# Sixteen head pairs of a sparse attention in one hand order for all engines: two full-array visits per pair, K and Q rows cast once and placed by DMA between SBUF tiles

## The chip, the cores and the metric

The kernel runs on one core of one Trainium2 chip. The metric is device time in microseconds (us) of one execution. The engines are named as in the profile: PE is TensorE, DVE is VectorE, ACT is ScalarE, POOL is GpSimd and SP is the engine that only issues transfers.

## The reference

Attention with a selection of key chunks, then a mixture of experts with one expert per token. There are B=4 batches, H=8 heads, S=768 positions and D=64; 24 chunks of 32 keys, of which each query keeps six; E=8 experts with 512 to 1024 to 512 (N=3072 tokens).

```python
k_min = np.min(k_chunks, axis=3); k_max = np.max(k_chunks, axis=3)
ub = np.sum(np.maximum(q[..., None, :] * k_min, q[..., None, :] * k_max), axis=-1)
ub = np.where(causal, ub, -1e9)                 # by chunk
top_chunks = np.argsort(ub, axis=-1)[..., -6:]
scores = scale * q @ k.T
scores = np.where(sel & (i >= j), scores, -1e9) # sel: the chunk of j is kept
x = softmax(scores) @ v                         # [3072, 512] over all heads
logits = x @ w_gate
e = argmax(logits); g = softmax(logits)[e]
out = g * (relu(x @ w1[e]) @ w2[e])
```

## The kernel before

**Pairs.** The 32 heads are worked as NP=16 pairs; pair i is pair hp = i % 4 of batch b = i // 4. `load` brings q, k and v of a pair (fp32, 128 positions on the partitions). PE transposes K and Q so that the two heads lie on partitions 0 to 63 and 64 to 127. From K's transposes DVE takes each chunk's maximum and minimum (`kmx`, `kmn`), and `kse` makes their sum and difference (`KS`, `KD`). ACT writes K, scaled, into `KTE` as bf16, once for each head and half. `q_e` copies Q's transposes to `qT`, their absolute value to `qA`, and casts them into the rows 0 to 63 of `QSB`, head 0 on POOL and head 1 on ACT.

**Selection.** `ub` multiplies `KS` by `qT` and `KD` by `qA` (fp32, in 64-column tiles), which gives the upper bound of each chunk. Its transposes go to DVE (`select`), which takes the eight largest of each list with `max` and marks in `nsel` what is not among the six. `mask` transposes `nsel`, and ACT puts it in rows 64 to 87 of `QSB`. Rows 64 to 87 of `KTE` hold an indicator of the chunk, so one bf16 matmul over the whole array gives scores that are already masked.

**Scores and attend.** Scores are made transposed (keys on the partitions), in seven units u0 to u6: u0 and u1 are the first 384 queries, u2 to u6 the second 384. Each unit is one `scores` (PE, then exp on ACT into a tile `Pa` or `Pr`, then, on the diagonal, affine selects on POOL, L300) and one `attend` (PE, P times V into halves of 64 columns, fp32). DVE adds the units' P up in `acc` (L325), and copies the output `po` to `ot` (L318).

**Denominators and router.** `ud` of a pair (L341 and L346, 32-column tiles) makes from `acc` the softmax's denominators and from `ot` the pair's share of the router's logits. `lgp` transposes and divides these, `sums` adds the shares in `lg` on POOL, and `xr` transposes `ot`, scales it and writes it, as bf16, to `xrow`. After the last pair of a batch `route_steps` follow in the pairs of the next batch: `logits` (DVE), `rank` (PE and DVE), and six `scatter`s (POOL, indirect DMAs, L443) that write tokens to `xs_dram` by expert.

**Experts.** NA=11 tiles of 128 tokens are known early (`table`, over pairs 13 and 14), 28 tiles in all run. Each tile is gathered (POOL, L542), turned by a DMA transpose (`x_in`) into one of six slots in KTE[0] and QSB[0], then `up` (8 matmuls, Relu L592, a DMA transpose of h), and `down` (8 matmuls), scaling and an indirect DMA to the output. The second four gathers each reuse a buffer of the first four, whose transposes they wait for. The weights come as 32 pieces of 512 KB that POOL's queue casts to bf16 (`load_w`, L166).

**Order.** PE, POOL and SP run in the order in which the code lists instructions; DVE and ACT are left to the tile scheduler, apart from the start and from the last pair on, where they too run in the listed order. Within a pair there are four groups: scores u2 and u3; u4 and u5; u6; and, for the next pair, u0 and u1. After the scores of each group come the attends of the group before. `ub` follows the first group, `select` the second, `mask` the third and `lgp` and `x0` the fourth. The spread of scatters is a list, one or two to a group:

```python
spread = ((), (0,), (2, 4), (1,), (3, 5), (), (), ())
```

In the last pair the order of POOL is gathers 0 to 3, the affine selects of the groups as they come, and gathers 4 to 7 after scores u6.

## Time and profile before

| | |
|---|---|
| time, median of 3 executions | 370.18 us (369.44 to 373.85) |
| the profiled execution: its time | 363.95 us |
| the profiled execution: its span | 362.1 us |
| mean granted PE clock | 0.988 |
| busy PE / DVE / ACT / POOL | 93% / 64% / 65% / 49% |
| DMA packets, bytes, mean rate | 138215, 59.83 MB, 165 GB/s |
| first scores / first `up` | 16.73 us / 248.81 us |
| weight pieces, time from issue to landing (median) | 6.0 us |

The page has one row per engine of the busy share, with the number of instructions. In the slices each digit is the busy share of one fortieth of the span, in tenths, and PEclk is the clock that PE was granted. The profiled execution's time is that span with 1.85 us around it.

### The profile page before, as it was taken

What the parts mean: (1) busy time and instruction counts of PE and PEld (TensorE: products, weight loads), DVE (VectorE), ACT (ScalarE), POOL (GpSimd) and SP (SyncE); (2) the same over time, 40 slices, a digit from 0 to 9 for tenths busy, and PEclk for the clock granted to TensorE, in tenths of its full rate; (3) what the DMA queues carried; (4) which work ended last, traced back from release to release, by engine and by line L of the source; (5) the groups of instructions that cost most, each with busy time, mean ns of one, the idle gap of its engine ahead of it and who ended that gap; (6) DMA issues with size and microseconds to landing.
All of it is one profiled execution on the core that took longest, in us unless ns stands there. A gap on an engine that the chain in (4) does not pass through costs nothing. (4 is left out here: it accounts for less than half of the span.)

```text
span 362.1 us, 7547 instructions
## 1 busy us (share of the span) xinstructions
PE 335.4 (93%) x2312; PEld 173.4 (48%) x2312; DVE 232.1 (64%) x811; ACT 235.2 (65%) x398; POOL 177.1 (49%) x296
## 2 busy tenths in 40 slices
PE   6777999999999999999999997998999899999990
PEld 5534455465554554554545544443544344444440
DVE  5789788898998898998988999775370010000000
ACT  2496797797887977977879778462354445544450
POOL 3074333452476343457424538375576765555331
PEclk9999999999999999999999998999999999999996
DMA  7619997999948989957989992366999999999841
GB/s 148 114 24 198 201 206 113 217 194 177 219 108 185 191 121 195 205 123 193 167 138 201 183 186 67 83 125 121 164 193 236 204 245 211 215 197 193 175 123 51
DMA packets 138215, 59.83 MB, mean 165 GB/s; under 512 B 122811, under 2 KB 131005, under 8 KB 138176
## 3 DMA queue, kind: packets, MB, share of 16 engines
q1 hardware_dynamic: 119072, 29.52, 45.9%
q0 software_dynamic: 17536, 29.42, 42.0%
q10 hardware_dynamic: 1568, 0.39, 0.6%
q8 instruction: 21, 0.34, 0.4%
q14 instruction: 18, 0.15, 0.1%
HBM read 56.14 MB, written 10.51 MB: 184 GB/s over the span
## 5 line engine op out<-in xcount | busy, mean ns | idle before, releaser
L325 DVE TENSOR_TENSOR Pa<-Pa,Pr 128x768 f32<-128x768 f32 (+2 forms) x112 | 81.5, 728 | 1.8 <-DVE Pa L325 0.5
L300 POOL TENSOR_SCALAR_AFFINE_SELECT Pr<-Pr 128x256 f32<-128x256 f32 x80 | 31.9, 418 | 76.2 <-ACT Pr L296 75.3
L296 ACT ACTIVATE Pr<-ps 128x768 f32<-128x768 f32 (+2 forms) x112 | 65.0, 628 | 3.2 <-PE ps L291 2.9
L600 PE MATMUL py<-w_all,hT 128*128 x224 | 52.6, 379 | 1.0 <-DMA hT<-h__4066 0.8
L291 PE MATMUL ps<-QSB,KTE 128*128 128x384 bf16 (+2 forms) x288 | 49.1, 294 | 1.7 <-ACT QSB L265 1.2
L542 POOL DMA_INDIRECT xg<-xs_dram,grow x28 | 29.9, 1068 | 22.6 <-DVE gt_all L565 7.4
L563 DVE TENSOR_TENSOR ti_all<-xg,inv_i 128x1 int32<-128x1 int32 x17 | 2.8, 163 | 58.0 <-DMA xg<-xs_dram,grow 58.0
L291 PEld LDWEIGHTS <-KTE 128*128 128x128 bf16 x288 | 24.2, 98 | 32.6 <-issue 25.3
L608 POOL DMA_INDIRECT out_dram<-y,ti_all x28 | 27.8, 994 | 24.4 <-ACT y L607 18.7
L600 PEld LDWEIGHTS <-hT 128*128 128x128 bf16 x224 | 21.8, 98 | 27.6 <-DMA hT<-h__4066 1.2
L607 ACT ACTIVATE y<-py,gt_all 128x512 f32<-128x512 f32 x27 | 18.5, 687 | 20.6 <-PE py L600 19.9
L349 ACT ACTIVATE ud<-pu 128x384 f32<-128x384 f32 x16 | 7.9, 492 | 36.5 <-PE pu L346 36.5
L443 POOL DMA_INDIRECT xs_dram<-xrow,sli x24 | 26.9, 1121 | 6.6 <-issue 4.5
L589 PE MATMUL ph<-w_all,KTE 128*128 x120 | 28.4, 379 | 0.0
L296 ACT ACTIVATE Pa<-ps 128x768 f32<-128x768 f32 x32 | 26.0, 813 | 2.9 <-PE ps L291 2.3
L166 POOL DMA_DIRECT2D w_all<-in_moe_w_dram x32 | 24.4, 762 | 0.0
L300 POOL TENSOR_SCALAR_AFFINE_SELECT Pa<-Pa 128x256 f32<-128x256 f32 x16 | 6.5, 405 | 36.5 <-ACT Pa L296 36.5
L589 PE MATMUL ph<-w_all,QSB 128*128 x96 | 22.7, 379 | 0.2 <-issue 0.2
L379 DVE TENSOR_TENSOR xrow<-pt,rec 128x384 bf16<-128x384 f32 x32 | 17.6, 552 | 3.0 <-PE pu L236 1.7
L204 DVE TENSOR_REDUCE kmx<-pt 128x12 f32<-128x384 f32 x30 | 16.7, 556 | 4.0 <-PE pt L202 3.9
L221 POOL CAST QSB<-qT 64x384 bf16<-64x384 f32 x30 | 16.7, 564 | 4.1 <-DVE qT L219 2.7
L318 DVE COPY ot<-po 128x384 f32<-128x384 f32 x32 | 17.7, 553 | 1.2 <-PE po L313 1.2
(306 smaller groups left out, 639.5 us busy)
## 6 DMA issues: line engine op xcount, KB each, us to landing
w_all<-in_moe_w_dram POOLq DMA_DIRECT2D x32, 512.0 KB, 6.0
xg<-xs_dram,grow POOLq DMA_INDIRECT x28, 3.9
out_dram<-y,ti_all POOLq DMA_INDIRECT x28, 4.3
t__122<-in_k_dram SPq DMA_DIRECT2D x2, 192.0 KB, 3.5
t__125<-in_q_dram ACTq DMA_DIRECT2D x2, 192.0 KB, 4.0
t__128<-in_v_dram SPq DMA_DIRECT2D x2, 192.0 KB, 5.6
t__196<-in_k_dram SPq DMA_DIRECT2D x2, 192.0 KB
t__206<-in_q_dram SPq DMA_DIRECT2D x2, 192.0 KB, 3.7
```

Of the source, the lines that this page charges most:

```text
L166: nc.gpsimd.dma_start(out=dst, in_=src.rearrange("(c p) f -> p c f", p=128))
L291: nc.tensor.matmul(pv[:, hd, :], lhsT=kte[:, hd, ts(kb, 128)], rhs=qsb[:, hd, ds(qb * 384 + 384 - w, w)], start=True, stop=True, skip_grou ...
L296: nc.scalar.activation(P[:, :, ds(c0, w)], pv, AF.Exp)
L300: nc.gpsimd.affine_select(out=pd, in_=pd, pattern=[[0, 2], [1, 128]], compare_op=ALU.is_ge, fill=0.0, base=0, channel_multiplier=-1)
L318: nc.vector.tensor_copy(out=ot[:], in_=po[:])
L325: nc.vector.tensor_tensor(acc[:, :, 384 - w:384], acc[:, :, 384 - w:384], P[:, :, ds(c0, w)], ALU.add)
L443: d = nc.gpsimd.indirect_dma_start(out=xs_dram[:], out_offset=bass.IndirectOffsetOnAxis(ap=sli[:, u:u + 1], axis=0), in_=bst[b][f"xrow{u % ...
L542: d = nc.gpsimd.indirect_dma_start(out=xg_bufs[j % XB][:].bitcast(I32), out_offset=None, in_=xs_dram[:], in_offset=bass.IndirectOffsetOnAx ...
L589: nc.tensor.matmul(ph[:, fh, :], lhsT=xT[:, c, :], rhs=w_all[:, ds(wo + (c * F + fh * 512), 512)], start=(c == 0), stop=(c == NDC - 1), sk ...
L600: nc.tensor.matmul(py[:], lhsT=hT[:, c, :], rhs=w_all[:, ds(wo + (W1W + c * DM), DM)], start=(c == 0), stop=(c == NFC - 1))
L607: nc.scalar.activation(y[:], py[:], AF.Copy, bias=0.0, scale=fs[j]["gt"])
L608: d = nc.gpsimd.indirect_dma_start(out=out[:], out_offset=bass.IndirectOffsetOnAxis(ap=fs[j]["ti"], axis=0), in_=y[:], in_offset=None, bou ...
```

## The change

All five engines now run in one order that a function `iteration(i)` writes out. In an iteration, PE works on the scores of pair i, on u6's attend and the router's part of pair i-1, on the selection of pair i+1, and on the transposes of pair i+2. Scores u0, u1, u4 and u5 are split in two tiles of 64 columns (`split`), so that with the attends and `ub` they are of one mode; the whole array is used from q's transposes to u3, and from the masks to the transposes of x.

K and Q are cast once for both heads: K on ACT to `kB`, Q on POOL to `qB`; `rows` copies them by DMA to rows 0 to 63 of `KTE` and `QSB` (four DMAs per pair, on SP's queue). `kse` goes from DVE to POOL, the copy of the second output to ACT, and the exps of a unit of two parts become one. `ub` and the masks cover only the queries from 128 on (640 of 768); the earlier ones see at most four chunks and keep them all. Of the PSUM pools, the first output moves to `ps_m` and K's transposes to `ps_s`. `Pr` has three buffers, not four. The constants of the second set of buffers are made at the start, the rest of them (`consts_last`) in iteration 0. In the start, K and Q of the first pair are loaded over two queues, v later.

The early table is made at once, in iteration 14. `logits` and `rank` of a batch stand in its successor's second iteration, and three scatters each in the second and third, ahead of the affine selects of u6 and of `kse`. In the last iteration gathers 4 to 7 stand ahead of u6's affine selects. The pieces of weights follow the list `npiece`, two of them in the start; w2's rows lie so that a partition gets one row of 4096 bytes, and the Relu of `up` reads PSUM with a stride of four elements to match.

The core of the diff:

```diff
+        nc.gpsimd.memset(KS[1][:], 0.0)
+        nc.gpsimd.memset(KD[1][:], 0.0)
+        nc.gpsimd.memset(QSB[1][64:128], 0.0)
+        nc.gpsimd.tensor_copy(out=KTE[1][64:128], in_=KTE[0][64:128])
...
     def consts_last():
-        nc.gpsimd.memset(KS[1][:], 0.0)
-        nc.gpsimd.memset(KD[1][:], 0.0)
-        nc.gpsimd.memset(QSB[1][64:128], 0.0)
-        nc.gpsimd.tensor_copy(out=KTE[1][64:128], in_=KTE[0][64:128])
...
-        nc.gpsimd.dma_start(out=dst, in_=src.rearrange("(c p) f -> p c f", p=128))
-
-    late, sums_ = [], []
-
-    def flush(*qs):
-        for q_ in qs or (sums_, late):
-            for f_ in q_:
-                f_()
-            q_.clear()
+        nc.gpsimd.dma_start(out=dst, in_=src.rearrange("(c p) f -> p c f" if n < 2 else "(p c) f -> p c f", p=128))
...
+    def k_ev(i, hf):
+        if hf == 1:
+            st[i]["kB"] = work.tile([128, S], BF16, tag="kB", name="kB")
+        d = nc.scalar.activation(st[i]["kB"][:, ts(hf, 384)], st[i]["pk"][hf], AF.Copy, bias=0.0, scale=0.125)
...
+    def rows(i, nm, dst):
+        for hd in range(2):
+            nc.sync.dma_start(out=dst[i % 2][0:64, hd, :], in_=st[i][nm][64 * hd:64 * hd + 64, :])
+
+    def kse(i, eng):
+        s = st[i]
+        for hd in range(2):
+            r = slice(64 * hd, 64 * hd + 64)
+            c = slice(32 * hd, 32 * hd + NCH)
+            eng.tensor_tensor(KS[i % 2][r, c], s["kmx"][r, :], s["kmn"][r, :], ALU.add)
+            eng.tensor_tensor(KD[i % 2][r, c], s["kmx"][r, :], s["kmn"][r, :], ALU.subtract)
...
+    def q_T(i, hf):
+        nc.vector.tensor_copy(out=st[i]["qT"][:, hf], in_=st[i][f"pq{hf}"][:])
+
+    def q_A(i, hf):
+        nc.scalar.activation(st[i]["qA"][:, hf], st[i][f"pq{hf}"][:], AF.Abs)
+
+    def q_c(i):
+        st[i]["qB"] = work.tile([128, S], BF16, tag="qB", name="qB")
+        for hf in range(2):
+            nc.gpsimd.tensor_copy(out=st[i]["qB"][:, ts(hf, 384)], in_=st[i]["qT"][:, hf])
+
+    def ub_mm(i):
+        s = st[i]
+        pu = ps_m.tile([128, 384], FP32, tag="m", name="pu")
+        for w_, nm in ((KS, "qT"), (KD, "qA")):
+            x_ = s[nm][:].rearrange("p a c -> p (a c)")
+            for h in range(2):
+                nc.tensor.matmul(pu[64 * h:64 * h + 64, 0:320], lhsT=w_[i % 2][:],
+                                 rhs=x_[:, ds(128 + 320 * h, 320)],
+                                 start=(nm == "qT"), stop=(nm == "qA"), skip_group_check=True)
+        s["pu"] = pu
...
+    def mask_ev(i, pt):
+        for hd in range(2):
+            nc.scalar.activation(QSB[i % 2][64:64 + NCH, hd, 128:S], pt[32 * hd:32 * hd + NCH, 128:S], AF.Copy)
...
+    def s_mm(i, u, split=False):
         kte, qsb = KTE[i % 2], QSB[i % 2]
         qb, parts = units[u]
         ps = ps_s.tile([128, 2, 512], FP32, tag="s", name="ps")
+        for kb, w, c0 in parts:
+            for hd in range(2):
+                for h in range(2 if split else 1):
+                    n = 64 if split else 128
+                    nc.tensor.matmul(ps[ds(h * n, n), hd, ds(c0, w)], lhsT=kte[:, hd, ds(kb * 128 + h * n, n)],
+                                     rhs=qsb[:, hd, ds(qb * 384 + 384 - w, w)],
+                                     start=True, stop=True, skip_group_check=True)
+        st[i][f"ps{u}"] = ps
...
+    def o_ev(i, qb):
+        ot = work.tile([128, 384], FP32, tag="ot", bufs=3, name="ot")
+        if qb == 0:
+            nc.vector.tensor_copy(out=ot[:], in_=st[i]["po0"][:])
         else:
-            acc = s[f"acc{qb}"]
-            for n, (kb, w, c0) in enumerate(parts):
-                nc.vector.tensor_tensor(acc[:, :, 384 - w:384], acc[:, :, 384 - w:384],
-                                        P[:, :, ds(c0, w)], ALU.add)
+            nc.scalar.activation(ot[:], st[i]["po1"][:], AF.Copy)
+        st[i][f"ot{qb}"] = ot
...
-            nc.scalar.activation(h_[:], ph[:], AF.Relu)
+            nc.scalar.activation(h_[:].rearrange("q a (c p) -> q a c p", c=4),
+                                 ph[:].rearrange("q a (p c) -> q a c p", c=4), AF.Relu)
...
+    npiece = [3, 3, 3, 3, 3, 0, 2, 2, 2, 0, 2, 2, 3, 0, 2, 2]
+    assert sum(npiece) == 4 * E
+    wnext = iter(range(4 * E))
+
+    def pieces(i, n):
+        for _ in range(min(n, npiece[i])):
+            load_w(next(wnext))
+            npiece[i] -= 1
...
+    def q_prep(i):
+        q_mm(i, 0)
+        q_mm(i, 1)
+        if i + 1 < NP:
+            load(i + 1, "q")
+        q_T(i, 0)
+        q_A(i, 1)
+        q_T(i, 1)
+        q_A(i, 0)
+
+    def k_prep(i, two):
+        k_mm(i, two)
+        if i + 1 < NP:
+            load(i + 1, "k")
+        k_red(i, 0)
+        k_ev(i, 1)
+        k_red(i, 1)
+        k_ev(i, 0)
+
+    def iteration(i):
+        p, n, m = i - 1, i + 1, i + 2
+        b, hp = divmod(i, HP)
+        last = i == NP - 1
+        router = hp == 1 and b > 0
+        rt = rout.get(p)
+        for u in (0, 1):
+            s_mm(i, u, i > 0)
+            s_ex(i, u)
+        if i > 1:
+            rout[i - 2]["sums"]()
+        if i == 0:
+            k_prep(1, False)
+            kse(1, nc.gpsimd)
+            q_prep(1)
+            q_c(1)
+            rows(1, "kB", KTE)
+            rows(1, "qB", QSB)
+        else:
+            av(p, 6)
+            if not last:
+                load(n, "v")
+            o_ev(p, 1)
+            add(p, 6)
+            if router:
+                route[b - 1][0]()
+            if n < NP:
+                ub_mm(n)
+                ub_ev(n)
+            if m < NP:
+                q_prep(m)
+            if n < NP:
+                sel_mm(n)
+                sel_v(n)
+        if last:
+            for j in range(XB):
+                gather(j)
+                x_in(j)
+        if i == NP - 2:
+            for _ in early_table:
+                pass
+        for u in (2, 3):
+            s_mm(i, u)
+            s_ex(i, u)
+        if router:
+            route[b - 1][1]()
+        pieces(i, 2)
+        av(i, 0)
+        av(i, 1)
+        add(i, 1)
+        o_ev(i, 0)
+        if i == 0:
+            ub_mm(1)
+            ub_ev(1)
+        for u in (4, 5):
+            s_mm(i, u, True)
+            s_ex(i, u)
+        if 0 < i and m < NP:
+            q_c(m)
+        pieces(i, 1)
+        if router:
+            route[b - 1][2]((0, 2, 4))
+        if hp == 2 and b > 0:
+            route[b - 1][2]((1, 3, 5))
+        av(i, 2)
+        av(i, 3)
+        add(i, 3)
+        add(i, 4)
+        if i == 0:
+            consts_last()
+            sel_mm(1)
+            sel_v(1)
+            q_prep(2)
+            q_c(2)
+        elif n < NP:
+            mask_ev(n, mask_mm(n))
+        if i > 0:
+            rt["ud_mm"]()
+            rt["ud_ev"]()
+        s_mm(i, 6)
+        if last:
+            for j in range(XB, 2 * XB):
+                meta(j - XB)
+                gather(j)
+                if j < len(x_slots):
+                    x_in(j)
+        if m < NP:
+            rows(m, "qB", QSB)
+        s_ex(i, 6)
+        if i == 0:
+            av(i, 4)
+            mask_ev(1, mask_mm(1))
+        add(i, 5)
+        if m < NP:
+            k_prep(m, True)
+            rows(m, "kB", KTE)
+            kse(m, nc.gpsimd)
+        if i > 0:
+            rt["lgp_mm"]()
+            rt["lgp_v"]()
+            for hf in range(2):
+                rt["x_mm"](hf)
+            for hf in range(2):
+                rt["x_v"](hf)
+        if i > 0:
+            av(i, 4)
+        av(i, 5)
...
+    with tc.manual_schedule(engines={PE, POOL, SP, DVE, ACT}):
+        first_pair()
...
+            iteration(i)
         rt = rout[NP - 1]
         r = route[B - 1]
+        rout[NP - 2]["sums"]()
+        av(NP - 1, 6)
+        o_ev(NP - 1, 1)
+        add(NP - 1, 6)
```

## The prediction

> **What bounds the kernel now.** I read five views in this order: busy shares, slices, the windows of single pairs, the timelines of TensorE and GpSimd inside one pair, and the groups. The chain that ended last says nothing here: all its shares are 0%.
>
> ```profile
> PE 335.4 (93%) x2312; PEld 173.4 (48%) x2312; DVE 232.1 (64%) x811; ACT 235.2 (65%) x398; POOL 177.1 (49%) x296
> ...
> PE   6777999999999999999999997998999899999990
> ...
> POOL 3074333452476343457424538375576765555331
> PEclk9999999999999999999999998999999999999996
> ```
>
> TensorE is busy in almost every slice and no other engine comes near it, so TensorE sets the time. The attention half runs from the first scores at 16.73 us to the first `up` at 248.81, the MoE tail from there to 362.1. In the attention half the denominators (L341/L346) of successive pairs start 14.19 us apart. The windows between such starts (us, then busy time and count of PE, weight load, DVE, ACT, POOL, then clock, DMA share, GB/s):
>
> ```profile
> 42.56:56.75 14.19, 14.12 (x112) 7.56 (x108) 12.38 (x39) 11.64 (x21) 4.88 (x11) 1.00 1.09 188
> 99.72:113.92 14.20, 14.11 (x113) 7.56 (x108) 13.17 (x40) 11.66 (x21) 10.73 (x16) 1.00 0.59 149
> 214.74:232.56 17.82, 15.79 (x112) 8.17 (x108) 15.25 (x56) 11.81 (x21) 10.69 (x16) 0.90 0.26 73
> ```
>
> A plain pair and a routing pair take the same 14.2 us: the three scatters of the second window (POOL 10.7 instead of 4.9 us) cost nothing, because GpSimd has room and they stand apart. Only pair 13, with the early table on DVE and a clock of 0.90, is longer. Inside a pair, TensorE's starts (start, duration; ends are modelled):
>
> ```profile
> 106.57 0.82 PE L291 MATMUL ps<-QSB,KTE 128*128 128x384 bf16 x4
> 107.37 0.55 PE L377 MATMUL pt<-ident_f,ot 128*128 128x128 f32 x3
> 107.85 0.87 PE L313 MATMUL po<-Pa,t__1450 128*64 128x384 f32 x4
> 108.55 0.82 PE L313 MATMUL po<-Pr,t__1450 128*64 128x256 f32 x8
> ```
>
> A bf16 384-wide matmul streams 162 ns, an fp32 group of four 64-column ones 645, a transpose 110. Adding these up, a pair streams 12.3 us. The other 1.9 us are gaps: 94 to 100 ns when the array goes from whole to 64 columns, 102 to 153 back, 100 from 64 to 32, 116 from 32 to whole, and 0.3 where the transposes of `xr` wait for a PSUM buffer. A pair goes to the whole array four times.
>
> The scatters and gathers on GpSimd will decide the forecast:
>
> ```profile
> 109.58 1.00 POOL L443 DMA_INDIRECT xs_dram<-xrow,sli  x1 [0.16 <-issue]
> 110.88 1.08 POOL L443 DMA_INDIRECT xs_dram<-xrow,sli  x1 [0.30 <-issue]
> ...
> 239.59 1.08 POOL L542 DMA_INDIRECT xg<-xs_dram,grow  x1 [0.36 <-POOL Pr L300]
> ...
> 245.56 1.13 POOL L300 TENSOR_SCALAR_AFFINE_SELECT Pr<-Pr 128x256 f32<-128x256 f32 x3
> 247.87 1.02 POOL L542 DMA_INDIRECT xg<-xs_dram,grow  x1 [1.18 <-DVE gt_all L565]
> ...
> 254.31 1.01 POOL L542 DMA_INDIRECT xg<-xs_dram,grow  x1 [0.30 <-issue]
> ```
>
> Scatters in a row are 1.30 us apart, and land 2.6/4.1/5.8 us (min/median/max) after issue. The gathers 0 to 7 of the last pair take from 239.59 to 255.3, 15.7 us, because each of the second four waits for what a first one feeds. The diagonal's affine selects of the last pair (245.56) stand ahead of that second four.
>
> [...] The trace shows a cold stretch of 3.4 us at 218.45. [...] No scatter here landed in less than 2.6 us.
>
> **The change part by part.** T is the start of an iteration's first scores.
>
> TensorE's own work. Two of four round trips between whole and 64 columns go: 2 x (97 + 128) = 0.45, and with the slower first matmul after each (51 ns) 0.55. `ub` streams 320 instead of 384 columns: -0.215 from its two 645-ns groups. The PSUM wait of 0.3 goes, since lgp and x are apart and two tiles moved to other pools. Splitting u0, u1, u4, u5 into 64-column tiles lets them share the 64-column mode; weight loads hide beside matmuls today, I put 0.09 on the 128-wide parts. Sum: 14.19 - 0.55 - 0.215 - 0.3 + 0.09 = 13.2; summing the new order group by group gives 12.96 to 13.06. I take 13.06. Bounds 12.9 and 13.6, the latter if the split tiles' extra weight loads show.
>
> The other engines at 13.06. ACT: `L222`'s evictions go, four half-height K casts become two; `o_ev(1)` comes, and two small exps per pair merge: about 10.2 us. DVE loses kse and one copy of the output: about 11.1. GpSimd gets kse (4 small ones) and a second full cast: about 7.4. The row DMAs on SP (four of 98 KB per pair) add 0.4 MB to 1.2 MB of q, k, v and up to 1.6 MB of weights per pair, and in iterations 0 to 4 three weight pieces stand each, against two or three. The DMA share of the first window is 1.09 already (packets overlap, so it may exceed 1). Rows are issued half a pair before their use and q, k, v a whole one: price 0, and up to 3 in each of four iterations if DMA is the limit there. Everything fits, but one loop is tight: ub, q's transposes, DVE's copies and selection, the K reductions, kse on GpSimd, ub again adds up to about 12.4, so slack is only some 0.6. Anything that delays kse by more is paid in full.
>
> Iteration 0. The DVE part of `consts_last` stands ahead of `sel_v(1)` and waits for iotas that GpSimd makes behind two weight pieces and affine selects (about 27.6). Then mask and its eviction follow at 31, so T1 = 33.5 instead of 30.3: 17.2 for this iteration, 14.0 without the stop. T0 is about 16.35, since both loads are split over two queues (-0.4).
>
> Routing iterations, first kind (5, 9, 13). `logits` waits for GpSimd's sums, which now stand behind the affine selects of u1 (T + 3.5); behind it in DVE's order are q's copies, behind its exp on ACT is ub's eviction: +2.6. Three scatters in a row (3 x 1.30) stand ahead of the affine selects of u6 and of kse: +1.5. In the built program kse's third operation waits for the landing of the same three scatters: from T + 16.7 to T + 19.4 at 2.7 us, near the shortest landing: +1.6 more. So 18.76, a stop of 5.7. Bounds 0 (sums early, landing inside the slack) and 7.5 (a landing of 5.8).
>
> Second kind (6, 10). Scatters T + 9.8 to 13.5, landing 16.5, ub of the next iteration must follow: 15.8, a stop of 2.75, bounds 0 and 5.
>
> Iteration 14: the three table parts together, on DVE between selection and u1's add, 2.9; before, pair 13 paid 3.6 for the same with its cold clock. The same scatters stand there too.
>
> Last iteration. All eight gathers now stand on GpSimd ahead of the affine selects of u6. Gather 0 goes at about T15 + 3.9; plus 15.7, the selects at T15 + 19.6, attend of u6 at 20.4, `up(0)` at 21.2. Free of it: 10.9. Before: 12.2. A stop of 10.3, [...] add one cold stretch: 3.4 us at half clock costs 1.7. Bounds 5 (gathers' waits were partly caused by other work before) and 12.
>
> Tail. From `up(0)` to the end it was 113.3. The stall at 250.63 (ud waits DVE's adds, 2.4 with the gap to 252.95) goes, since DVE has finished in the wait: -2.4. The new w2 layout makes Relu read PSUM in stride of four. No row shows that. Relu is 1.02 us in a tile of 3.454 and runs ahead by three tiles, so even doubling it is hidden: 0. At 2.7 times it would decide, up to +10; a gain from the longer rows of w2 is bounded by its DMA share, and the weights are not waited for: 0.
>
> The sum. Without stops: T0 -0.4; fifteen iterations 14.0 + 14 x 13.06 = 196.8 against 219.9 before (16.73 to 236.6): -23.1; last 10.9 against 12.2: -1.3; tail -2.4. Together -27.2. Stops: 3.2 + 3 x 5.7 + 2 x 2.75 + 2.9 + 10.3 + 1.7 = 40.7. Net +13.5: a span of 375.6. The profiled execution was 363.95 at span 362.1 (1.85 around it), so 377.45 on that scale; the median of the runs shown, 370.18, is 1.017 of it. So 384.
>
> **Rivals.** The gain of 27 us rests on many small gaps, all visible; what differs is how many stops bite. The break-even is at 27 of 40.7 us; a measurement of this kernel can tell about 2% from no change, 7.4 us, so it is faster below 20 us of stops, the same up to 34.5.
>
> First rival, the other side: TensorE stays the bound, iterations run at 13.06, for the one reason that waits on GpSimd end inside the slack: landings near 2.6, sums ready, gathers faster than 15.7 as they no longer compete with four affine selects. For it: GpSimd is idle for half of the span, and scatters cost nothing before. Against: before, nothing of the loop stood behind them. With 12 us of stops left (half of the last, 3 of i14, one of the rest): 362.1 - 27.2 + 12 = 346.9, times 1.017 with the 1.85: 355.
>
> Second: the stops are about two thirds, gain and stops cancel: kse of plain iterations in time, routing iterations at +3.3 and +1.3, iteration 0 +1, the last one +8.5, cold clock and table as above: 27.1, so 0 net: 370. For it: several stops overlap with each other in one iteration.
>
> Third, slower still: DMA limits iterations 1 to 4 (4 x 3 = 12), on top of the stops. A pair's q, k and v take the 16 DMA engines 6.5 us and a weight piece 3.2, so 6.5 + 3 x 3.2 + some 1.5 for the rows is 17.6 against 13.06; what speaks against is that 16.1 fitted into 14.19 before. Span 387.6: 396.
>
> **How the numbers follow.** Chances: the forecast 0.52, the third 0.12, the second 0.22, the first 0.14. Slower by over 2%: 0.64; within: 0.22; faster: 0.14. The range goes from 360 (8 us above the first rival's own centre, leaving about 1 in 10 below) to 400 (DMA or iterations of 13.6, with landings of 5.8).
>
> **What would show it.** Right: iterations without routing 13.0 to 13.2 apart; 5, 9, 13 near 18.8; kse's third operation waiting on the scatters; in the last iteration a hole of about 9 us on TensorE with the gathers on GpSimd in it, then half clock. Wrong: routing iterations as long as the others, u6's affine selects not late in the last, plain iterations over 13.6 (in 1 to 4: DMA), or the tail's tiles away from 3.454.

## The result and the profile after

The changed kernel takes 404.43 us (median of four executions, 403.22 to 406.79) against 369.81 of the kernel before (369.44 to 373.85). The ratio of the means is 1.0917, 95% interval 1.0822 to 1.1012: slower by 9%, where 4%, and 384 us, had been forecast. The profiled execution of the changed kernel took 403.22 us at a span of 401.2, 39.1 over the 362.1 of before. Beside some of the later runs the kernel before took 364 us and beside others 370, so differences of some 6 us between single spans say nothing, and iterations are compared instead.

From the page of the changed kernel (busy, then slices of PE, POOL and the granted clock):

```profile
PE 339.9 (85%) x2458; PEld 190.3 (47%) x2468; DVE 222.2 (55%) x735; ACT 207.1 (52%) x322; POOL 210.5 (52%) x356
...
PE   7677996997959599788889977976697999899994
...
POOL 7156555446464545455736527376637456465322
PEclk9898999999969699996969999799899699999999
```

PE does nearly the same work, but eight points less of the span are busy, and the clock falls in several slices of the attention half, not in one. Windows of single iterations (columns as in the prediction's windows; the borders are the first scores of successive pairs, so these are iterations 2, 3, 5, 6, 7 and the last but one):

```profile
49.00:61.99 12.99, 12.97 (x121) 8.24 (x119) 11.70 (x35) 9.69 (x16) 8.45 (x16) 1.00 1.11 201
61.99:80.49 18.50, 14.49 (x120) 8.89 (x118) 12.22 (x36) 9.68 (x16) 8.91 (x18) 0.91 1.09 206
...
93.47:109.41 15.94, 13.76 (x133) 8.38 (x130) 13.94 (x51) 9.82 (x17) 7.17 (x14) 1.00 0.88 153
109.41:129.28 19.87, 15.33 (x121) 9.17 (x119) 11.91 (x35) 9.90 (x16) 10.96 (x19) 0.83 0.73 154
129.28:149.34 20.06, 15.72 (x121) 9.30 (x119) 12.25 (x35) 9.99 (x16) 10.84 (x21) 0.83 0.73 155
...
246.09:266.97 20.88, 14.80 (x108) 7.58 (x106) 13.62 (x51) 8.26 (x12) 10.31 (x18) 0.84 0.52 114
```

A plain iteration is what was hoped for: 12.99 us, PE busy for 12.97, against 14.19 before. All the loss is in the others. In 6 and 7 the engines do no more than in 2, but for three scatters on GpSimd (PE's 2.4 to 2.8 us more are half clock: the granted clock is 0.83 there, 1.00 in 2), so they wait. The waits of the whole run (engine, line, for what: us in total, times, longest):

```profile
DVE xrow L415 <- DMA xs_dram<-xrow,sli: 12.2, 3, 5.0
...
PE pu L250 <- POOL KS L222: 8.6, 5, 2.5
...
POOL KS L222 <- DMA xs_dram<-xrow,sli: 7.7, 5, 2.4
...
PE pq L185 <- DMA q_t<-in_q_dram: 5.3, 3, 4.0
```

`ub` (L250) waits five times for `kse`, and `kse` five times for scatters to land (the landing is the end of a transfer in the profile). Iterations 5 and 6, GpSimd and then PE:

```profile
110.86 0.97 POOL L477 DMA_INDIRECT xs_dram<-xrow,sli  x1 [0.30 <-issue]
111.84 0.77 POOL L323 TENSOR_SCALAR_AFFINE_SELECT P<-P 128x256 f32<-128x256 f32 x2
112.58 0.23 POOL L222 TENSOR_TENSOR KS<-kmx,kmn 64x24 f32<-64x24 f32 x1
112.77 0.23 POOL L223 TENSOR_TENSOR KD<-kmx,kmn 64x24 f32<-64x24 f32 x1
115.36 0.23 POOL L222 TENSOR_TENSOR KS<-kmx,kmn 64x24 f32<-64x24 f32 x1 [2.36 <-DMA xs_dram<-xrow,sli]
```

```profile
112.31 0.87 PE L337 MATMUL po<-P,v_t 128*64 128x256 f32 x8 [2.08 <-issue]
115.65 1.34 PE L250 MATMUL pu<-qT,KS 128*64 128x320 f32 x4 [2.46 <-POOL KS L222]
116.77 1.28 PE L250 MATMUL pu<-qA,KD 128*64 128x320 f32 x4
117.98 1.54 PE L185 MATMUL pq<-ident_f,q_t 128*128 128x128 f32 x6
```

The scores of the pair began at 109.41. u6's attend comes at 112.31 because the affine selects stood behind three scatters, `ub` at 115.65 because the last scatter had to land; then a group of four takes 1.34 us instead of 0.71, since the granted clock is 0.50 from 113.14 to 119.97. The same landing holds DVE at `xrow`:

```profile
115.33 0.56 DVE L415 TENSOR_TENSOR xrow<-px,rec 128x384 bf16<-128x384 f32 x1 [4.97 <-DMA xs_dram<-xrow,sli]
```

The last pair (GpSimd, then PE): gathers 4 to 7 end at 283.87, then come the affine selects, and the attend of u6 at 284.36, after 5.70 us of idle PE.

```profile
278.85 1.02 POOL L577 DMA_INDIRECT xgqT<-xs_dram,grow  x1 [1.69 <-DMA KTE<-xgqT]
...
282.87 1.00 POOL L577 DMA_INDIRECT xgqA<-xs_dram,grow  x1 [0.38 <-issue]
283.89 0.77 POOL L323 TENSOR_SCALAR_AFFINE_SELECT P<-P 128x256 f32<-128x256 f32 x2
```

```profile
284.36 1.55 PE L337 MATMUL po<-P,v_t 128*64 128x256 f32 x8 [5.70 <-POOL P L323]
```

The 39.1 us by stretches, from the starts of first scores and the first `up` in both timelines: start -0.2, fifteen iterations 250.5 against 219.9 (+30.6), last pair to `up(0)` 18.9 against 12.2 (+6.7), tail 115.3 against 113.3 (+2.0).

### The profile page after: what moved, and what is told of

It reads as the page before. It is cut to its first block, busy times and chain, and to the rows that moved or that the text cites. A ratio compares the mean times of both kernels' runs of the same rounds, so it can differ in the third digit from the quotient of the medians.

```text
span 401.2 us, 7848 instructions
## 1 busy us (share of the span) xinstructions
PE 339.9 (85%) x2458; PEld 190.3 (47%) x2468; DVE 222.2 (55%) x735; ACT 207.1 (52%) x322; POOL 210.5 (52%) x356
## 3 DMA queue, kind: packets, MB, share of 16 engines
q0 software_dynamic: 11392, 29.42, 34.8%
## 5 line engine op out<-in xcount | busy, mean ns | idle before, releaser
L319 ACT ACTIVATE P<-ps 128x768 f32<-128x768 f32 x112 | 87.4, 811 | 42.7 <-PE ps L306 31.3
L337 PE MATMUL po<-P,v_t 128*64 128x384 f32 (+2 forms) x576 | 88.1, 431 | 15.9 <-issue 9.9
L323 POOL TENSOR_SCALAR_AFFINE_SELECT P<-P 128x256 f32<-128x256 f32 x96 | 45.5, 497 | 99.8 <-ACT P L319 91.3
L345 DVE TENSOR_TENSOR P<-P 128x768 f32<-128x768 f32 (+2 forms) x112 | 84.4, 753 | 16.7 <-POOL P L323 4.4
L337 PEld LDWEIGHTS po<-P,v_t 128*64 128x64 f32 x576 | 39.1, 140 | 48.1 <-issue 33.0
L306 PE MATMUL ps<-QSB,KTE 128*128 128x384 bf16 (+3 forms) x442 | 50.9, 301 | 0.9 <-ACT P L319 0.9
L306 PEld LDWEIGHTS <-KTE 128*128 128x128 bf16 (+1 forms) x442 | 31.3, 109 | 23.8 <-issue 18.8
L242 POOL CAST qB<-qT 128x384 bf16<-128x384 f32 x30 | 33.8, 1151 | 3.6 <-DVE qT L234 3.5
L234 DVE COPY qT<-pq 128x384 f32<-128x384 f32 x30 | 16.3, 555 | 28.1 <-PE pq L185 23.3
L644 ACT ACTIVATE y<-py,gt_all 128x512 f32<-128x512 f32 x27 | 18.6, 687 | 23.6 <-PE py L637 16.5
L237 ACT ACTIVATE qA<-pq 128x384 f32<-128x384 f32 x30 | 13.5, 488 | 19.5 <-PE pq L185 12.2
L415 DVE TENSOR_TENSOR xrow<-px,rec 128x384 bf16<-128x384 f32 x32 | 16.5, 549 | 12.2 <-DMA xs_dram<-xrow,sli 12.2
L185 PE MATMUL pq<-ident_f,q_t 128*128 128x128 f32 x96 | 17.2, 324 | 6.2 <-DMA q_t<-in_q_dram 5.3
L250 PE MATMUL pu<-qT,KS 128*64 128x320 f32 x64 | 14.6, 540 | 8.9 <-POOL KS L222 8.6
L292 ACT ACTIVATE QSB<-pm 24x640 bf16<-24x640 bf16 x30 | 20.8, 693 | 1.4 <-PE pm L286 0.9
```

What stands on the lines that cost most here:

```text
L242: nc.gpsimd.tensor_copy(out=st[i]["qB"][:, ts(hf, 384)], in_=st[i]["qT"][:, hf])
L292: nc.scalar.activation(QSB[i % 2][64:64 + NCH, hd, 128:S], pt[32 * hd:32 * hd + NCH, 128:S], AF.Copy)
L306: nc.tensor.matmul(ps[ds(h * n, n), hd, ds(c0, w)], lhsT=kte[:, hd, ds(kb * 128 + h * n, n)], rhs=qsb[:, hd, ds(qb * 384 + 384 - w, w)], s ...
L319: nc.scalar.activation(P[:], ps[:, :, 0:384], AF.Exp)
L323: nc.gpsimd.affine_select(out=pd, in_=pd, pattern=[[0, 2], [1, 128]], compare_op=ALU.is_ge, fill=0.0, base=0, channel_multiplier=-1)
L337: nc.tensor.matmul(po[64 * hd:64 * hd + 64, 384 - w:384], lhsT=vt[:, kb, hd, :], rhs=P[:, hd, ds(c0, w)], start=first, stop=last and n == ...
```

## The experiments

All are edits of the changed kernel unless said otherwise. "It k" is iteration k, from first scores to first scores. Spans are of one profiled execution each. A row is three scatters one behind the other; rows stand in iterations 5, 6, 9, 10, 13 and 14, and what one holds up shows in the iteration after it. c3 to c6 and e9 stand in the text alone.

| run | span | it 0 | 1 | 3 | 5, 6, 7 | 9, 10, 11 | 13, 14 | last | tail |
|---|---|---|---|---|---|---|---|---|---|
| changed | 401.2 | 18.3 | 14.3 | 18.5 | 15.9, 19.9, 20.1 | 15.9, 19.1, 19.8 | 15.9, 20.9 | 18.9 | 115.3 |
| a2_changed_again | 396.8 | 18.4 | 14.3 | 19.3 | 16.0, 19.7, 19.8 | 16.0, 19.4, 19.8 | 16.0, 22.7 | 19.4 | 107.6 |
| e1_kse_dve | 389.2 | 24.9 | 14.5 | 14.1 | 16.0, 17.6, 15.1 | 16.8, 15.9, 15.1 | 16.3, 21.4 | 18.9 | 108.4 |
| e2_x1late | 395.5 | 18.2 | 14.3 | 18.5 | 15.6, 21.1, 19.8 | 15.6, 19.6, 19.5 | 15.6, 21.8 | 19.4 | 108.0 |
| e3_both | 384.2 | 22.7 | 14.5 | 18.8 | 17.4, 15.5, 15.2 | 17.4, 15.5, 15.2 | 16.0, 18.9 | 20.7 | 108.4 |
| e4_sums | 392.4 | 18.4 | 14.4 | 18.6 | 15.0, 20.8, 19.9 | 15.0, 20.0, 18.1 | 15.0, 23.0 | 18.1 | 107.9 |
| e5_pieces | 393.2 | 16.9 | 16.7 | 13.0 | 16.0, 19.7, 20.0 | 16.0, 19.2, 19.6 | 15.9, 24.9 | 19.7 | 107.6 |
| e6_gathers | 395.4 | 22.4 | 14.5 | 19.8 | 16.0, 20.4, 20.0 | 15.9, 19.4, 19.7 | 16.0, 21.1 | 12.1 | 110.5 |
| e7_consts | 395.7 | 15.8 | 16.5 | 18.5 | 16.0, 19.6, 19.8 | 16.0, 19.3, 19.7 | 16.0, 21.4 | 19.1 | 109.8 |
| e8_scatter_place | 378.1 | 22.1 | 14.5 | 17.0 | 16.3, 13.7, 13.1 | 16.4, 13.7, 13.0 | 16.4, 17.9 | 19.1 | 113.6 |
| c1_all | 360.9 | 16.7 | 15.1 | 13.1 | 15.1, 15.7, 14.1 | 15.3, 15.7, 14.4 | 16.5, 20.5 | 11.6 | 109.2 |
| c2_early | 366.5 | 16.7 | 16.7 | 13.0 | 16.4, 13.7, 13.3 | 19.8, 13.6, 13.0 | 19.1, 13.2 | 12.8 | 115.6 |
| c7_mid | 366.5 | 16.6 | 16.7 | 13.1 | 16.7, 15.1, 16.9 | 16.7, 14.5, 17.6 | 16.7, 14.7 | 13.3 | 108.8 |

### Which wait holds the routing iterations

```diff
-            kse(m, nc.gpsimd)
+            kse(m, nc.vector)
```

> kse of the later pairs goes back from GpSimd to DVE; nothing else changes. Theory A (kse's third operation on GpSimd waits for the landing of the scatters, and ub of the next iteration waits for kse): iterations 6, 7, 10, 11 and 14 now take 19.9, 20.1, 19.1, 19.8 and 20.9 us against 12.98 of a plain one; all five lose 5 to 7 us, in sum 27 to 33, and the span is 368 to 374. Rival B (the same landing holds DVE's second xrow write in iterations 5, 9 and 13, and with it the adds, q's copies and the selection behind it): only 7 and 11 gain, 12 to 14 us, and 6, 10 and 14 stay at about 19; span 387 to 389. In both, plain iterations stay within 0.3 us of 12.98, since DVE has 1.3 us of room for 0.9 us more.

Iterations 6, 7, 10, 11 and 14 lost 2.3, 5.0, 3.2, 4.7 and -0.5, together 14.7 us, which lies between the two: the wait of `kse` was most of the stop in 7 and 11, and something else keeps most of 6, 10 and 14. Its waits have no line for `kse` and a landing any more, while `xrow` still waits:

```profile
DVE xrow L415 <- DMA xs_dram<-xrow,sli: 10.3, 3, 4.6
```

Iteration 0 became 6.7 us longer: PE waited 8.8 us for q's load of pair 2. It is as long in three other runs (e3, e6, e8), so it isn't the edit. The eight runs without weight pieces in the start (e5, c1 to c7) don't have it, so full DMA in the start is likely, but not shown by itself. The stop of iteration 3 was in iteration 4 here (19.1, which the table leaves out; PE waited 4.5 us there for q).

```diff
+        if hp == 2 and b > 0:              # behind u3 of it 6, 10, 14
+            rout[i - 2]["x_mm"](1)
+            rout[i - 2]["x_v"](1)
         for u in (4, 5):
...
-            for hf in range(2):
+            hfs = (0,) if router else (0, 1)
+            for hf in hfs:
                 rt["x_mm"](hf)
-            for hf in range(2):
+            for hf in hfs:
                 rt["x_v"](hf)
```

> In iterations 5, 9 and 13 the second half of x (its transposes and DVE's write to xrow) is put off to the next iteration, behind u3, so that DVE no longer stands at a wait for scatters; kse stays on GpSimd. Theory A: no gain (within 2 us of span 401), since kse still waits for the landing. Rival B: iterations 6, 10 and 14 fall from about 20 to about 13, in sum 18 to 21 us, span 380 to 383.

No gain in 6, 10 and 14 (62.4 against 59.9), as theory A says: while `kse` waits, DVE's wait at `xrow` adds nothing.

Both edits together, `kse(m, nc.vector)` and the later second half of x:

> Both edits: kse on DVE and the second half of x put off. Theories A and B together: no engine of the loop waits for a landing, so iterations 6, 7, 10, 11 and 14 are at 13 to 14.5 us (14 with the early table at 14 to 16), in sum 28 to 34 us less, span 367 to 373. If a third cause holds them (GpSimd's time for three scatters in a row, 3.9 us, ahead of u6's affine selects), they stay at 15 to 16.

With no engine of the loop waiting for a landing, 6, 7, 10 and 11 took 15.2 to 15.5, still 2.1 to 2.5 over this run's plain iteration of 13.08. That is the third cause: in each of the four, u6's attend waits 1.8 to 2.0 us for the affine selects that stand behind the row. The five iterations gave 19.5 us and 5, 9 and 13 took 2.9 back.

The place of the scatters, and the router's parts ahead of them:

```diff
+        def weights():                     # split off the logits' part: exp and what follows
             ex = work.tile([128, 6, E], FP32, tag="ex")
...
+            if hp == 0 and b > 0:          # end of it 4, 8, 12
+                rt["sums"]()
+                route[b - 1][0]()
...
-            add(p, 6)
             if router:
-                route[b - 1][0]()
+                route[b - 1][3]()          # weights
+            add(p, 6)
...
+            if router:                     # right behind ub
+                route[b - 1][1]()
+                route[b - 1][2]((0, 2, 4))
+            if hp == 2 and b > 0:
+                route[b - 1][2]((1, 3, 5))
...
-        if router:
-            route[b - 1][2]((0, 2, 4))
-        if hp == 2 and b > 0:
-            route[b - 1][2]((1, 3, 5))
```

> Only the router's place is changed in the changed kernel: sums and logits at the end of iterations 4, 8, 12 (the weights' exp behind the exps of u1), rank and three scatters right behind ub in 5, 9, 13, three in the same place in 6, 10, 14. kse stays on GpSimd, and all other stops stay. If the place of the scatters ahead of kse is the whole cost: iterations 5, 6, 7 together fall from 55.9 to 41 to 43 us, 9 to 11 from 54.8 alike, 13 and 14 from 36.8 to 31 to 33, span 366 to 374. If the logits chain itself costs (11 small operations on DVE): 5, 9 and 13 stay at 15 or more, span 374 to 382.

Iterations 6, 7, 10 and 11 fell to 13.0 to 13.7 with `kse` still on GpSimd, and the five lost 28.3 us. The wait views of this run list no wait of `kse` or `xrow` for a scatter and none of `ub` for `kse`. The logits and the rank moved too in 4 and 5, but in 6 only the second row did, and 7 fell from 20.1 to 13.1. So the cause is the place of a row, late in the iteration, with u6's affine selects, `kse` and `xrow` behind it; e1 and e3 show how it divides.

Iterations 5, 9 and 13 stayed at 16.4, and 4 and 8 took 1.3 and 1.6 more. The expectation put this down to the logits' chain, but the trace does not: in 4 and 8 PE waits 1.2 and 1.6 us for q's load, and 12, with the same chain, took 12.99. In 5, 9 and 13 the selection's transposes wait 1.6 us for `base_e`, the last operation of the rank, and the rank's first matmul 0.6 us for the logits' result.

```diff
-        for u in (0, 1):
-            s_mm(i, u, i > 0)
-            s_ex(i, u)
         if i > 1:
             rout[i - 2]["sums"]()
+        for u in (0, 1):
+            s_mm(i, u, i > 0)
+            s_ex(i, u)
```

> The sums of the router's shares stand on GpSimd ahead of u1's affine selects instead of behind them, in every iteration; all else as in the changed kernel. Prediction's step: iterations 5, 9 and 13 lose their stop of about 2.95 us before logits, from 15.94 to 13.2 to 14, span 6 to 9 us less (392 to 395). Rival (the stop is the length of the 11 small DVE operations of logits, 1.9 us, ahead of q's copies): from 15.94 to 14.7 or more, span at most 4 less.

5, 9 and 13 fell to 15.0, so the wait for the sums was 1.0 of 2.95; the other 2.0 fit the rival, the chain itself. The next ones took it back: 20.8 and 20.0 in 6 and 10 (14 took 23.0, but 22.7 in the unaltered kernel's second profile).

The other direction, in the kernel before:

```diff
-    spread = ((), (0,), (2, 4), (1,), (3, 5), (), (), ())
+    spread = ((), (), (0, 2, 4), (), (), (), (1, 3, 5), ())
```

> The kernel before, with its scatters in two rows of three (one row in each of two successive pairs) instead of spread out; nothing else. There kse is on DVE and the second xrow write stands two groups later. If a row of three is costly by itself (3.9 us of GpSimd ahead of affine selects): six rows lose 1.5 us or more each, span 371 or more. If it costs only where kse or an xrow write stands behind it: within 3 us of 362.

The span was 372.7, but of the 10.6 us more 4.8 are in the tail and 1.7 in the start. Of the periods between denominators, that of the first row grew from 14.2 to 15.9, those of the next three rows by 0.0 to 0.2 each, and the last three by 2.0 in sum. In the first row's iteration an xrow write waited 1.9 us for a landing, the only such wait in this run. Where nothing of the loop waits behind it, a row of three costs little.

### DMA, the last pair, the start

```diff
-    npiece = [3, 3, 3, 3, 3, 0, 2, 2, 2, 0, 2, 2, 3, 0, 2, 2]
+    npiece = [0, 2, 2, 2, 2, 2, 2, 2, 3, 2, 2, 2, 3, 3, 3, 0]
```

> Of the changed kernel only the list of weight pieces is changed: none in the start and in iteration 0 (five before), two in each of 1 to 7 (three in 1 to 4, none in 5), the rest later. Theory D (DMA is the limit in iterations 0 to 4: the third rival of the prediction; q's load of iteration 3 was 4 us late): iteration 3 falls from 18.5 to 13 to 14, iteration 1 from 14.3 to 13 to 13.5, and none of the first five shows a wait for q's load; 6 to 7 us in sum. Rival (the load of q is late because SP's queue holds it behind the row DMAs, not because DMA is full): iteration 3 stays at 17 or more.

Iteration 3 fell to 12.99: full DMA (a share of 1.09 there in the changed kernel), not SP's order. No run without pieces in the start has a stop there. Iteration 1 did not gain; 0 and 1 together took 33.6 us against 32.5, and in 1 PE waits for ACT and not for q, as in the changed kernel. So what is over 13 in iteration 1 is not shown to be DMA. 14, with three pieces beside its scatters, took 24.9 (20.9 and 22.7 in the two profiles of the changed kernel).

```diff
         s_mm(i, 6)
         if last:
+            s_ex(i, 6)
             for j in range(XB, 2 * XB):
...
-        s_ex(i, 6)
+        if not last:
+            s_ex(i, 6)
```

> In the last iteration u6's exps and affine selects stand ahead of gathers 4 to 7 on GpSimd, as in the kernel before. Prediction's step (u6's attend waits for the gathers): from the last pair's first scores to up(0) it takes 18.9 us; it falls by 5.7 to 8, to 11 to 13. Rival (up(0) waits for its gathered tokens or for ud anyway): it falls by under 3.

It fell by 6.8, from 18.9 to 12.1: the step is confirmed. Its tail took 110.5, against 107.6 in the second profile of the changed kernel, so some of it may come back there.

```diff
         if i == 0:
-            consts_last()
             sel_mm(1)
             sel_v(1)
+            consts_last()
```

> In iteration 0 consts_last stands behind the selection instead of ahead of it. Prediction's step (selection on DVE waits behind operations that wait for an iota on GpSimd): iteration 0 falls from 18.25 by 2.5 to 3.5 us. Theory D as a rival: the load of q for pair 2 becomes the limit there and it falls by under 1.

Iteration 0 fell by 2.5, as its step said, and iteration 1 rose by 2.3: the stop was moved, not removed. In the start the next stop is close behind.

### All together, and single parts of it

The edits of e4 (sums first), e6, e7 and the `npiece` list of e5, with these:

```diff
-        if router:
-            route[b - 1][2]((0, 2, 4))
-        if hp == 2 and b > 0:
-            route[b - 1][2]((1, 3, 5))
...
+        if hp == 2 and b > 0:              # second half of x, now ahead of u6's exp
+            rout[i - 2]["x_mm"](1)
+            rout[i - 2]["x_v"](1)
...
-            kse(m, nc.gpsimd)
+            kse(m, nc.vector)
+        if router:                         # scatters at the end, behind all casts
+            route[b - 1][2]((0, 2, 4))
+        if hp == 2 and b > 0:
+            route[b - 1][2]((1, 3, 5))
...
+            hfs = (0,) if router else (0, 1)
```

> All edits together: kse on DVE, scatters behind kse at the end of iterations 5, 6, 9, 10, 13 and 14, the second half of x put off in iterations 5, 9, 13, sums early, selection ahead of consts_last, fewer early weight pieces, u6's affine selects ahead of gathers 4 to 7. If these stops are all there is: iterations 1 to 13 at 13.0 to 14.0, iteration 0 at 14 to 15, 14 at 15 to 16, last 11 to 13, tail 108 to 113; span 328 to 340, 6 to 9% under the kernel before. If moving a stop only shows the next one (scatters now delay u1's affine selects; DVE gets fuller by kse): iterations 5 to 7 and so on stay at 15, span 345 to 355.

Neither: 360.9, and 0.998 of the kernel before (0.996 to 1.000), 20 executions against 21. The stops of iteration 3 and the last pair are gone, and no wait for a landing is listed. 14 stayed at 20.5, where the early table still stands, and 5 and 6 at 15.1 and 15.7.

Next, the places of e8 (its exp still in the logits' part) with the edits of e6 and e7, another list of pieces, and the early table behind u5's add:

```diff
-    npiece = [3, 3, 3, 3, 3, 0, 2, 2, 2, 0, 2, 2, 3, 0, 2, 2]
+    npiece = [0, 2, 2, 2, 2, 2, 2, 3, 3, 2, 2, 3, 3, 2, 2, 0]
...
-        if i == NP - 2:
-            for _ in early_table:
-                pass
         for u in (2, 3):
...
         add(i, 5)
+        if i == NP - 2:
+            for _ in early_table:
+                pass
...
         av(i, 5)
+        if i == NP - 3:
+            next(early_table, None)
```

> The scatters go into the hole that GpSimd has in every iteration between u1's affine selects and u5's: sums and logits stand at the end of iterations 4, 8, 12, rank and three scatters right after ub in the next one, the other three in the same place of the one after. kse stays on GpSimd. Selection ahead of consts_last, no early weight pieces, the early table in the last part of iterations 13 and 14, u6's affine selects ahead of gathers 4 to 7. If the stops came from where the scatters and waits stood: iterations 5 to 14 at 13.0 to 14.5, last 11.5, tail 108 to 110, span 330 to 342. If GpSimd's order can't hide them: iterations 5 and 6 at 15 or more, span over 350.

6, 7, 10, 11 at 13.0 to 13.7 and 14 at 13.2 (the early table stands behind the adds there, and costs nothing), but 5, 9 and 13 at 16.4, 19.8 and 19.1; ratio 0.9956 (0.9931 to 0.9980). In all three ACT stands 2.7 us at the router's exp, which waits for DVE ahead of the exps of u0 and u1; in 9 and 13, which are 3.4 and 2.7 us longer than 5, PE also waits 3.2 and 3.7 us for q's load.

```profile
148.21 0.24 ACT L439 ACTIVATE ex<-sh 128x48 f32<-128x48 f32 x1 [2.67 <-DVE sh L427]
148.36 1.49 ACT L319 ACTIVATE P<-ps 128x768 f32<-128x768 f32 x2
```

c2_early with one edit more:

```diff
-            kse(m, nc.gpsimd)
+            kse(m, nc.vector)
```

> As c2_early, with kse on DVE. If kse's wait for landings (issued 5 us earlier now) still bites in c2_early, this one is 3 to 8 us faster; if the landings are over by then, it is within 2 us of it, or up to 3 slower because DVE has 0.9 us more per iteration.

Ratio 0.9891 (0.9856 to 0.9927), but it counts 12 of 21 executions, which scatter from 363.5 to 374.5. The medians of all are 368.1 here, 367.5 for c2_early and 369.8 for the kernel before. So both beat the kernel before by about 1% at most, and that `kse` on DVE adds to it isn't shown.

c2_early without the order of heads that saves the two visits:

```diff
         for u in (0, 1):
-            s_mm(i, u, i > 0)
+            s_mm(i, u)
...
         for u in (4, 5):
-            s_mm(i, u, True)
+            s_mm(i, u)
```

> As c2_early, but all scores over the whole array again (no 64-column tiles): four visits per pair instead of two. The prediction's term for the two visits saved is 0.55 less 0.09 per iteration: plain iterations 13.4 to 13.6 instead of 12.98, span 6 to 8 us more than c2_early. Rival (the iteration is bound by the loop over DVE and GpSimd, 12.4 to 12.9, and the visits are hidden): within 2 us.

Its plain periods (denominators to denominators) are 13.44, those of c2_early 12.99. The two visits saved are worth 0.45 an iteration; 0.46 was forecast. The span was only 2.1 over c2_early's; the routing iterations differ by waits that come and go, such as for q's load.

c2_early with w2 laid out as before:

```diff
-        nc.gpsimd.dma_start(out=dst, in_=src.rearrange("(c p) f -> p c f" if n < 2 else "(p c) f -> p c f", p=128))
+        nc.gpsimd.dma_start(out=dst, in_=src.rearrange("(c p) f -> p c f", p=128))
...
-                nc.scalar.activation(h_[:, fh].rearrange("q (c p) -> q c p", c=4),
-                                     ph[:].rearrange("q (p c) -> q c p", c=4), AF.Relu)
+                nc.scalar.activation(h_[:, fh, :], ph[:], AF.Relu)
```

> As c2_early, with w2's rows and the Relu as in the kernel before (four rows of 1024 bytes per partition, PSUM read without stride). Prediction: the layout is worth nothing, the tail from up(0) to the end stays within 1.5 us of c2_early's (some 109), and the Relu of a tile is 1.02 us in both. Rival (the layout shortens the tail by lighter DMA traffic): the tail is 113, as in the kernel before.

The tail was 119.7 against 115.6, but 4.2 us of it are slow register operations of PE, of which c2_early has none (see the end). The tail of the changed kernel itself varied by more, 107.6 to 115.3, so one execution each doesn't show whether the layout is worth something. Relu took 1.02 us with the stride in the changed kernel, as without it before: the stride costs nothing.

c2_early with the exp split off as in e8, and a list of pieces from the first iteration to the last:

```diff
-        pieces(-1, 2)
...
-    npiece = [0, 2, 2, 2, 2, 2, 2, 3, 3, 2, 2, 3, 3, 2, 2, 0]
+    npiece = [1, 2, 2, 2, 2, 2, 2, 2, 2, 2, 2, 2, 2, 2, 2, 3]
```

> As c2_early, with the exp of the router's weights split off from logits and put behind the exps of u1, and the weight pieces two to an iteration (one in iteration 0, three in the last, none in the start). In c2_early iterations 5, 9 and 13 took 16.4, 19.8 and 19.1: ACT stood 3 us at that exp and PE 3.3 at a late load of q. If these two are the cause: 5, 9, 13 at 13.5 to 14.5, span 345 to 352, 3 to 5% under the kernel before. If DMA can't take two pieces in 13 us together with q, k, v and rows: stops by q's load move to other iterations, span 355 to 365.

Ratio 1.0105 (1.0057 to 1.0152). 5, 9 and 13 took 17.2, 17.0 and 16.4 in the profiled execution (379.3 us; the median was 375.4), so the exp alone was not what held them: the selection's transposes wait 1.5 to 1.6 us for the rank. Weights arrived late in the tail (126.9; `up` waited 4.0 us for them).

c6_final with `kse` on DVE, the rank and the first row of scatters behind u3 instead of behind `ub`, and the pieces of e5:

```diff
-            if router:
-                route[b - 1][1]()
-                route[b - 1][2]((0, 2, 4))
...
+        if router:                         # behind u3's exp
+            route[b - 1][1]()
+            route[b - 1][2]((0, 2, 4))
```

> As c3_early_dve (kse on DVE, u6's affine selects ahead of gathers 4 to 7, early table late, selection ahead of consts_last), with the router's exp split off and put behind the exps of u1, rank and its three scatters behind u3 as in the changed kernel (before u4), and weight pieces as in c1_all (none in the start and iteration 0, three in 8, 12, 13, 14, two elsewhere). In c3_early_dve iterations 5, 9 and 13 took 16.7, 17.5 and 17.2, partly because rank's PSUM tile held up the selection. If that and the exp are the cause: 13.5 to 14.5 there, span 345 to 355 where the tail is 109 to 115, 2 to 5% under the kernel before. If DMA or DVE (now at 12.9 us of 13 with rank and weights) bound it: 15 to 16 there and no gain over c3_early_dve (0.989).

5, 9 and 13 at 16.7, no gain: 1.0110 (1.0078 to 1.0142). In each of the three PE waits 1.7 us at the rank for ACT's `qA`, and ACT there for DVE's copies of q, which stand behind the router's small operations: DVE, as the second half of the expectation said. 7 and 11 (16.9 and 17.6) waited 2.3 and 3.0 us for q's load. A version that has the gain of the plain iterations in 5, 9 and 13 too was not found.

The changed kernel itself once more:

> The changed kernel unaltered, profiled a second time. In its first profile PE's register operations of the tail took 0.7 us each instead of 0.05 in six places between 305 and 313 us, and the tail was 115.3 us. If these belong to the kernel, they are there again at the same tile, and the tail is 115; if they come and go from one execution to another, they are elsewhere or missing, and the tail is 108 to 112, with iterations 5 to 7 and 9 to 11 at 56 and 55 us as before.

The iterations repeated within 0.8 us except 14 (22.7), the tail was 107.6 and had no slow register operation.

## Why the prediction was wrong

**Right.** The bound and its new size: plain iterations 12.98 to 12.99 (13.06 forecast). Two visits less: 0.45 (0.46). That GpSimd's order makes it slower, and by which waits: `kse` for scatters, the sums, gathers 4 to 7, the constants of iteration 0. Iteration 0: 18.3 (17.2). The Relu's stride: no cost (1.02 us with it and without). The last pair had its hole in the forecast place, but smaller: 18.9 (22.9 with its cold stretch). The gathers took 12.8 us from first to last, not 15.7, probably because only one affine select stood between them (three before).

**The step that failed: the price of a row of scatters.** The sum had 3.1 us of scatter stop for a row in 5, 9 and 13 and 2.75 for one in 6 and 10, 14.8 together. Measured, beside a plain iteration: 6.9 and 7.1 in 6 and 7, 6.1 and 6.8 in 10 and 11, 7.9 in 14, of which about 4.9 in 14 are the early table (e8: 17.9; 13.2 in c2_early, where the table moved). That is some 30 us for five rows, 6 a row.

Iteration 6 adds up from its own trace. PE waits 2.1 us at u6's attend (1.5 forecast) and 2.5 at `ub` (1.6 forecast), and is busy 2.4 us longer at half clock, which was put at nothing: 6.9. The wait at `ub` was put too short: the landing came at 115.33, 4.5 us after the last scatter began (the sum took 2.7), and q's full casts ahead of the row took 1.2 us each, where those of half height took 0.56 before, so the row began later. The half clock was charged in the last pair alone, 1.7 us for its long hole; that only such a hole brings it was my estimate, which no trace had shown. Here it began at 113.14, between the holes of 2.1 and 2.5 us, and lasted 6.8 us. In the kernel before the cold stretch of 3.4 us lies at 223.6, not at 218.45 as I read it, and PE's longest hole ahead of it was 1.9 us. The landing also holds DVE's `xrow`. That adds nothing beside `kse`'s wait (e2).

**A case that was given too little: DMA.** Iteration 3 cost 5.5: 4.0 of waiting for q's load and 1.5 of half clock. This is the third rival's mechanism (12 us, chance 0.12), and e5 confirms it there. In the sum it was 0, for 16.1 of transfers had fitted into 14.19. Iterations 2 and 4, with three pieces as well, took 12.99, which fits a lateness that builds up over several iterations. Iteration 1 cost 1.3; why is open.

**Also short:** the early table 4.9 instead of 2.9. The logits' part, 2.6 for each of three, was 2.95. (The second rival's stops add up to 26.6, not 27.1, which changes nothing.)

**The sum.** 28.7 us of stops were forecast up to the last pair, 54.8 came (4.3 + 1.3 + 5.5 + 8.9 + 34.8). The difference of 26 is about the whole miss of the span, 401.2 against 375.6; the rest (start +0.1, plain iterations -1.1, last pair -4.0, tail +4.4) cancels, and that is luck: in the second profile the tail alone was 7.7 us shorter. Scaling by 1.017 was not sound either. It held for the kernel before, but the changed kernel's profiled execution was as slow as its other ones. So it was luck, too, that the forecast of 384 missed the median of 404 by 20 us, when its sum missed the profiled execution by 26.

## What to carry to other kernels

When instructions of an engine that runs in the listed order are put in a row, price what stands behind the last of them, and behind its landing, in the next iteration too; e8 gained 23 us of span by moving eighteen scatters, with the router's parts ahead of them, into a hole of the same engine. A gain of 1.2 us per iteration lowers the slack of everything else by as much: weight pieces that came in time at 14.19 us made q late at 12.99. Look at the granted clock beside PE's holes: those of iteration 6 are 4.5 us, and half clock added 2.4 (0.83 there, 1.00 in a plain iteration). And a wait that the program inserts should be looked for after an operation has changed its engine: `kse` had none for scatters on DVE.

## What was not expected of the hardware

The cast of 128 x 384 values on GpSimd (fp32 to bf16) took about 0.5 or about 1.2 us. In c1_all the two casts from 111.15 took 0.95 together, with DVE idle, and those from 98.47 took 2.39, with DVE in its fp32 additions:

```profile
98.47 2.39 POOL L242 CAST qB<-qT 128x384 bf16<-128x384 f32 x2
...
111.15 0.95 POOL L242 CAST qB<-qT 128x384 bf16<-128x384 f32 x2
```

```profile
97.30 3.20 DVE L345 TENSOR_TENSOR P<-P 128x768 f32<-128x768 f32 x3
...
112.78 0.56 DVE L350 COPY ot<-po 128x384 f32<-128x384 f32 x1 [2.98 <-PE px L410]
```

In the profile of the changed kernel all 27 casts that began while an addition ran took 1.21 to 1.24 us, and the other three 0.50 to 0.51. In the runs of the changed kernel and its edits, 429 of 434 casts that began while an addition ran took over 1.1 us, and each of these ended 0.36 to 0.37 us after that addition. Of the other 76, 75 took under 0.6 us, also where an addition began while they ran (49). So the traces show a wait for the addition that runs when the cast begins, and no slower rate; what makes the cast wait they do not show.

In some executions single register operations of PE take 0.66 to 0.70 us instead of 0.05 for a while in the tail. There are six at 305 to 313 us in the first profile of the changed kernel, none in its second and none in that of before, but four in e9, an edit of the kernel before; so they belong to neither kernel. PE's matmuls of one tile stand apart for nothing else:

```profile
308.81 0.38 PE L625 MATMUL ph<-w_all,KTE 128*128 x1 [0.85 <-issue]
309.57 0.38 PE L625 MATMUL ph<-w_all,KTE 128*128 x1 [0.38 <-issue]
310.93 0.43 PE L625 MATMUL ph<-w_all,KTE 128*128 x1 [0.98 <-issue]
```

The tail of the changed kernel was 115.3 us with them and 107.6 without. They take 4.2 us, and most of the rest goes with half clock (granted 0.50) from 311.1 to 317.9, right behind them. What causes them was not found.
